# A decode block (attention with a cached K and V, then a Mish MLP): query projection head by head, last output-projection group in 4+3+1 rows, mean from column sums first, bias in two bf16 parts

## The chip, the cores and the metric

One NeuronCore of a Trainium2 chip runs the whole program. The time is device time in microseconds (us) of one execution. The traces have one row of work for each engine: the tensor engine (PE), the vector engine (DVE), the scalar engine (ACT) and the sync engine (SP, which issues nearly all the DMAs); they also tell what ended an engine's idle time before an instruction. "PEld" is the loading of weights into PE.

A *ratio* below is the mean time of a kernel's fast runs over the mean time of the fast runs of the kernel before in the same rounds. It is therefore not quite the ratio of the medians that I quote.

## The reference, cut to what matters

```python
# x: (4,1,640); K, V: (4,32,4096,128) bf16; wq: (640,4096); wo: (4096,640); w1: (640,1728); w2: (1728,640)
def A(x, k_cache, v_cache, wq, wo):            # attention, one query per sequence
    q = (x @ wq) split into 32 heads of 128
    p = softmax(q . k_cache * 128**-0.5)
    return concat_heads(p . v_cache) @ wo
def B(x, w1, b1, w2):                          # MLP with Mish
    h = x @ w1 + b1
    return (h * tanh(softplus(h))) @ w2
h   = x + A(layernorm(x), ...)
out = h + B(layernorm(h), ...)
```

K and V are 134 MB each in bf16 and every byte is read once, so nearly all of the run is reading them.

## The kernel before: the parts that the change touches

There are 16 K tiles and 16 V tiles of 8.4 MB. They pass through three big SBUF slots, loaded from one DMA queue in program order. After the last V tile the queue brings wo (five loads), w1 (three) and w2 (four).

```python
# which rows of the weights come in one load
WOS = [(k, 0, G) for k in range(NHG - 1)] + [(NHG - 1, 0, G - 2), (NHG - 1, G - 2, G)]   # 8, 8, 8, 6, 2 rows
W1S = (0, 2, DC - 1, DC)                                                             # 2 + 2 + 1 rows
W2S = (0, 6, 10, 12, FM)
...
# head: query projection, 40 matmuls, then 128 small selection matmuls that spread q over partitions
for hg in range(NHG):
    for b in range(N):
        for g in range(G):
            mm(red[:, (2 + hg) % 4, b * Dh : (b + 1) * Dh],
               sel[r, b, SE - PG * g : SE - PG * g + P], q_all[r, g * Dh : (g + 1) * Dh],
               g == 0, g == G - 1, ("qb", hg) if done else None)
...
# tail, on PE: wo, then mean and mean of squares, then w1 with the bias put in as an fp32 matmul
wo_mm(0); o_mm(NT - 1); l_mm(hg); wo_mm(1); a_mm(hg); ...; wo_mm(2); wo_mm(3)    # -> y
pe.need("st")
for k in range(2):                       # k=0: y, k=1: y*y
    ...
    mm(s_ps[k], ones_d[:, :], st[:, k, :, :], True, True, ("s", k))
pe.need("cen")
for c0, c1 in zip(W1S, W1S[1:]):
    if c1 == DC - 1:
        pe.need("b1s")
        mm(red[:, 2, 0 : FC * N], ident_f[:, :], b1s[:, :, :], False, False)     # fp32
    pe.need(("w1", c0))
    ...                                  # 14 matmuls for each row c of w1
# tail, on DVE: st <- y; mu[k] <- sum over chunks of s_ps[k]; cen <- st - mu[0]; ...
```

In the tail, `wo_mm` are the matmuls with wo; `o_mm`, `l_mm` and `a_mm` finish the attention of the last heads for them. After w1 come a fixed chain (h1, exp on ACT, five DVE instructions, `act`), the w2 matmuls and the output.

The softmax here doesn't subtract the row's maximum and nothing guards it: scores larger than these inputs give would overflow.

## Time and profile before

| | before |
|---|---|
| median time | 663.01 us (4 runs, 662.70 to 663.21) |
| span of the profiled run | 661.1 us |
| bytes moved, mean rate | 283.5 MB, 429 GB/s |
| PE, DVE busy | 60%, 62% |
| last K or V, wo, w1, w2 loads landed | 634.89, 647.14, 652.55, 657.52 us |
| the three w1 parts landed | 649.26, 651.50, 652.55 us |

(A "landing" is the last of a load's completion events in the trace, from the span's start.)

The page of the kernel before: the span in 40 slices, then the chain that ended last.

```profile
DMA  9999999999999999999999999999999999999997
GB/s 390 437 444 440 441 417 420 441 436 442 433 436 416 444 436 432 436 440 420 436 436 436 436 436 440 416 444 433 432 440 436 420 440 432 432 440 440 408 420 293
...
## 4 chain that ended last, share of the span: by engine, by line
DMA 3%; PE 3%; DVE 0%; SPq 0%; issue 0%; ACT 0%
DMA slotB<-in_A_wo_dram 3%; PE red L708 1%; PE pv L708 1%; PE red L718 0%; PE y_ps L708 0%; SPq L250 0%; PE misc L708 0%; DVE tb L694 0%; DVE o_bf L704 0%; ACT ta L428 0%; DVE act L697 0%; DVE tb L683 0%; DVE h L671 0%; DVE tb L691 0%; DVE cen L633 0%
```

The DMA row is at 9 tenths in every slice but the last, and the rate stays between 408 and 444 GB/s between the first and the last slice. The transfers are the limit. The chain of waits reaches back to a DMA, the load of wo, and what follows it in the chain is the tail.

The timeline of the kernel before, from its last wo matmuls to the end of the w1 stage (start, length, engine, line, operation, output<-input; in brackets the engine's idle time before it and what ended that).

```profile
646.49 1.73 PE L708 MATMUL y_ps<-a_t,slotB 128*128 128x4 bf16 x40 [0.54 <-DMA slotB<-in_A_wo_dram]
648.26 0.18 DVE L613 COPY st<-y_ps 128x20 f32<-128x20 f32 x1 [4.49 <-PE y_ps L708]
...
648.49 0.62 PE L708 MATMUL misc<-st,ones_d 128*128 128x20 f32 x2 [0.27 <-DVE st L613]
...
648.94 0.59 PE L708 MATMUL pv<-st,ones_d 128*128 128x20 f32 x2
649.14 0.18 DVE L624 TENSOR_REDUCE mu<-misc 128x4 f32<-128x20 f32 x1 [0.50 <-PE misc L708]
649.36 0.18 DVE L633 TENSOR_TENSOR cen<-st,mu 128x20 bf16<-128x20 f32 x1
...
649.59 1.92 PE L708 MATMUL red<-cen,slotB 128*64 128x4 bf16 x28
...
651.37 0.66 PE L708 MATMUL red<-b1s,ident_f 128*128 128x56 f32 x2
...
651.96 2.95 PE L708 MATMUL red<-cen,slotB 128*64 128x4 bf16 x42
...
654.94 0.22 DVE L671 TENSOR_TENSOR h<-red,rstd 128x56 f32<-128x56 f32 x1 [4.26 <-PE red L708]
```

The last wo row landed at 647.14 us, but PE had been waiting since 645.94 for a load of six rows and started its 40 matmuls only at 646.49. The sums y are ready at 648.26. Then a copy, a matmul, a reduce and a subtract follow one another until the centred row `cen` is ready at 649.54. The w1 matmuls run without a gap from 649.59 to 654.91, with 0.64 us in between for the fp32 bias. PE never waits for w1: every part of it had landed before PE came to it.

### The profile page before, as it was taken

How to read it: one execution, taken by the hardware profiler on the slowest of the kernel's cores; microseconds unless marked ns; L12 is line 12 of the kernel's file. 1: busy time of each engine (PE TensorE's matmuls, PEld its weight loads, DVE VectorE, ACT ScalarE, POOL GpSimd, SP SyncE). 2: the span in 40 equal slices, each digit the busy share in tenths (PEclk: the TensorE clock that was granted, in tenths of full speed). 3: DMA queues.
4: the chain of work that ended last, by engine and by line, in shares of the span. 5: the costliest groups of instructions: out<-in, count | busy, mean ns of one | idle time of the engine just before them, and what ended most of it. 6: DMA issues, size and time to landing. Idle time of an engine off the chain costs nothing. (4 is left out here: it accounts for less than half of the span.)

```text
span 661.1 us, 5195 instructions
## 1 busy us (share of the span) xinstructions
PE 396.9 (60%) x2747; PEld 80.8 (12%) x1787; DVE 406.9 (62%) x252; ACT 41.6 (6%) x158; POOL 2.6 (0%) x14
## 2 busy tenths in 40 slices
PE   0856658568317595738407485838434656765767
PEld 0600000101101010101100010000110001010246
DVE  1077988386048779757218798849306798848612
ACT  0200000000000000000000000000000000000011
POOL 1000000000000000000000000000000000000000
PEclk9768787968658697958767887888876879797965
DMA  9999999999999999999999999999999999999997
GB/s 390 437 444 440 441 417 420 441 436 442 433 436 416 444 436 432 436 440 420 436 436 436 436 436 440 416 444 433 432 440 436 420 440 432 432 440 440 408 420 293
DMA packets 6978, 283.50 MB, mean 429 GB/s; under 512 B 1012, under 2 KB 1208, under 8 KB 2232
## 3 DMA queue, kind: packets, MB, share of 16 engines
q1 hardware_dynamic: 6640, 283.27, 99.2%
q8 instruction: 7, 0.11, 0.1%
q10 hardware_dynamic: 328, 0.09, 0.1%
q14 instruction: 3, 0.02, 0.0%
HBM read 283.35 MB, written 0.01 MB: 429 GB/s over the span
## 5 line engine op out<-in xcount | busy, mean ns | idle before, releaser
L515 DVE TENSOR_TENSOR slotA<-slotA,q_bc 128x8192 bf16<-128x8192 bf16 x32 | 140.6, 4416 | 104.3 <-DMA slotA<-in_A_k_cache_dram 104.3
L515 DVE TENSOR_TENSOR slotB<-slotB,q_bc 128x8192 bf16<-128x8192 bf16 x32 | 140.7, 4418 | 16.7 <-DMA slotB<-in_A_k_cache_dram 16.7
L526 DVE TENSOR_REDUCE s_f<-red 128x64 f32<-128x1024 f32 x64 | 78.0, 1219 | 97.7 <-PE red L718 97.6
L718 PE MATMUL red<-slotA,ident 128*128 128x512 bf16 x480 | 136.4, 447 | 0.0
L718 PE MATMUL red<-slotB,ident 128*128 128x512 bf16 x480 | 127.1, 424 | 0.0
L708 PE MATMUL red<-slotA,ident 128*128 128x512 bf16 x32 | 14.6, 456 | 118.9 <-PEq L49 118.9
L708 PE MATMUL pv<-slotC,e 128*32 128x512 bf16 x768 | 53.4, 439 | 36.9 <-PEq L49 33.9
L708 PE MATMUL red<-slotB,ident 128*128 128x512 bf16 x32 | 14.1, 440 | 87.5 <-PEq L49 87.5
L394 ACT ACTIVATE ex<-s_f 128x64 bf16<-128x64 f32 x64 | 16.4, 256 | 503.1 <-DVE s_f L526 503.1
L540 DVE TENSOR_TENSOR e<-ex,hmask 128x512 bf16<-128x512 bf16 x64 | 39.8, 684 | 0.0
L708 PEld LDWEIGHTS pv<-slotC,e 128*32 128x32 bf16 x768 | 22.7, 108 | 96.2 <-issue 82.9
L708 PEld LDWEIGHTS red<-slotA,ident 128*128 128x128 bf16 x32 | 3.2, 99 | 187.7 <-issue 187.6
L708 PEld LDWEIGHTS red<-slotB,ident 128*128 128x128 bf16 x32 | 3.1, 98 | 170.6 <-issue 170.6
L708 PEld LDWEIGHTS o_ps<-pv_sb,selo 128*32 128x32 f32 x136 | 13.5, 109 | 63.0 <-issue 62.9
L708 PE MATMUL o_ps<-pv_sb,selo 128*32 128x128 f32 x136 | 18.0, 276 | 0.0
L708 PE MATMUL pv<-slotA,e 128*32 128x512 bf16 x256 | 14.6, 380 | 0.4 <-PEq L49 0.4
L404 ACT COPY pv_sb<-pv 128x512 f32<-128x512 f32 x16 | 9.4, 586 | 70.4 <-PE pv L708 70.4
L394 ACT ACTIVATION_READ_ACCUMULATOR ex<-s_f 128x1 f32 x64 | 11.9, 186 | 0.0
L708 PE MATMUL red<-q_all,sel 32*128 32x128 bf16 x128 | 10.3, 273 | 0.8 <-PEq L49 0.8
L708 PEld LDWEIGHTS red<-q_all,sel 32*128 32x128 bf16 x128 | 10.1, 124 | 1.6 <-issue 1.6
L708 PEld LDWEIGHTS pv<-slotA,e 128*32 128x32 bf16 x256 | 7.0, 97 | 23.4 <-issue 17.7
L565 DVE RECIPROCAL rl<-misc 32x1 f32<-32x1 f32 x4 | 0.6, 151 | 14.3 <-PE misc L708 14.3
(96 smaller groups left out, 77.8 us busy)
## 6 DMA issues: line engine op xcount, KB each, us to landing
slotC<-in_A_v_cache_dram SPq DMA_DIRECT2D x2, 4096.0 KB, 40.6
slotC<-in_A_wq_dram SPq DMA_DIRECT2D x1, 5120.0 KB, 15.9
slotB<-in_A_wo_dram SPq DMA_DIRECT2D x3, 1280.0 KB, 17.7
slotB<-in_B_w_dram SPq DMA_DIRECT2D x2, 864.0 KB, 25.0
slotB<-in_A_wo_dram SPq DMA_DIRECT2D x1, 960.0 KB, 22.1
slotA<-in_B_w_dram SPq DMA_DIRECT2D x1, 960.0 KB, 25.2
slotA<-in_B_w_dram SPq DMA_DIRECT2D x1, 640.0 KB, 22.4
slotB<-in_B_w_dram SPq DMA_DIRECT2D x1, 432.0 KB, 26.4
```

Source lines behind the costliest of these rows:

```text
L394: lambda: a.activation(out=ex[:, sl], in_=s_f[:, sl], func=ACT.Exp, scale=SCALE, accum_out=rs[:, b, s : s + 1],),
L404: lambda: a.copy(out=pv_sb[:, :, :].rearrange("p r d -> p (r d)"), in_=pv[:, :]),
L515: lambda: v.tensor_tensor(out=t, in0=t, in1=q_bc[:, hg, b, :].unsqueeze(1).to_broadcast([P, RS, Dh]), op=ALU.mult,),
L526: lambda: v.tensor_reduce(out=s_f[:, s * RS : (s + 1) * RS], in_=red[:, k : k + 2, :].rearrange("p k (r c) -> p (k r) c", c=CW), axis=AX.X ...
L540: lambda: v.tensor_tensor(out=e[:, sl, :], in0=ex[:, sl].unsqueeze(2).to_broadcast([P, RS, G]), in1=hmask[:, :].unsqueeze(1).to_broadcast( ...
L565: dv.do(lambda: v.reciprocal(out=rl[:, :], in_=l_ps), ("rl", hg), DV)
L708: lambda: nc.tensor.matmul(out_, lhsT=lhsT, rhs=rhs, start=start, stop=stop, skip_group_check=skip),
L718: return t.add_instruction(mybir.InstMatmult(name=nc.get_next_instruction_name(), engine=mybir.EngineType.PE, ins=[t.lower_ap(rhs), t.lowe ...
```

## The change

The intent is to shorten the two places where the program is serial: the head (128 selection matmuls become 4) and the tail (a smaller last load of wo, one step less to the mean, a cheaper bias).

```diff
-    WOS = [...] + [(NHG - 1, 0, G - 2), (NHG - 1, G - 2, G)]
+    WOS = [...] + [(NHG - 1, a, b) for a, b in ((0, 4), (4, 7), (7, G))]
 # head: 40 projection matmuls write all heads into one bank; then
-        for hg in range(NHG):
-            for b in range(N):
-                for g in range(G):
-                    mm(red[:, (2 + hg) % 4, b * Dh : (b + 1) * Dh], sel[r, b, ...], q_all[r, ...], ...)
+        for b in range(N):
+            mm(red[:, (1 + b) % 4, :], sel[:, b * G : (b + 1) * G, :], q_all[:, :], True, True, ("qb", b))
 # tail, DVE
+        ysum <- tensor_reduce(y_ps over chunks)          # first, so that the mean needs no reduce afterwards
         st <- y_ps;  sq <- st * st
-        mu[0] <- tensor_reduce(s_ps[0]);  cen <- st - mu[0]
+        cen <- st - m_ps                                 # straight from PSUM
 # tail, PE
-            mm(s_ps[k], ones_d, st[:, k, :, :], ...)     # k = 0, 1
+        mm(m_ps, ones_d, ysum, True, True, "mean")
+        mm(sq_ps, ones_d, sq, True, True, "sqm")
-            if c1 == DC - 1:
-                mm(red[:, 2, ...], ident_f, b1s, ...)    # fp32, before the second w1 part
+            if c1 == DC:
+                for part in (b1_hi, b1_lo):              # b1s = b1_hi + b1_lo, both bf16
+                    mm(red[:, 2, ...], ident, part, ...) # before the last w1 part
```

More of the change, by code (lines that the diff above doesn't have):

```diff
@@ L121 @@
     book = Book()
-    WSEM = ["WQ", "WT"] + [f"W{k}" for k in range(12)]
+    WSEM = ["WQ", "WT"] + [f"W{k}" for k in range(13)]
     for s in ["PE", "DV", "DVP", "DVA", "AC", "ACP", "PO", "KA", "KB", "VA", "VC", "V2", "X", "S", "OUT0", "OUT1", "FIN"] + WSEM:
@@ L175 @@
     ln1 = sb("ln1", (N, D), BF16, setup, topC)
-    lnT = sb("lnT", (P, DC, QD), BF16, setup, topC)
+    lnT = sb("lnT", (P, DC, 2 * QD - N), BF16, setup, topC)
     xT = sb("xT", (P, DC, N), BF16, setup, topC)
-    q_all = sb("q_all", (P, QN), BF16, setup, topC)
-    SE = P - PG
-    sel_f = sb("sel_f", (P, N), FP32, setup, topC)
-    sel = sb("sel", (P, N, SE + P), BF16, setup, topC)
+    q_all = sb("q_all", (P, NHG * Dh), BF16, setup, topC)
+    sel_f = sb("sel_f", (P, N, G), FP32, setup, topC)
+    sel = sb("sel", (P, BG, PG), BF16, setup, topC)
     stats = sb("stats", (N, 2, nc.vector.BN_STATS_DIM), FP32, setup, topC)
@@ L192 @@
     ones_d = sb("ones_d", (P, P), FP32, tail, topA)
-    ident_f = sb("ident_f", (P, P), FP32, tail, topA)
     zeros = sb("zeros", (P, OC), BF16, tail, topA)
-    st = sb("st", (P, 2, DC, N), FP32, tail, topA)
-    mu = sb("mu", (P, 2, N), FP32, tail, topA)
+    ysum = sb("ysum", (P, N), FP32, tail, topA)
+    st = sb("st", (P, DC, N), FP32, tail, topA)
+    sq = sb("sq", (P, DC, N), FP32, tail, topA)
+    mu = sb("mu", (P, N), FP32, tail, topA)
+    esq = sb("esq", (P, N), FP32, tail, topA)
     cen = sb("cen", (P, DC, N), BF16, tail, topA)
@@ L202 @@
     b1s = sb("b1s", (P, FC, N), FP32, tail, topA)
+    b1_hi = sb("b1_hi", (P, FC, N), BF16, tail, topA)
+    b1_lo = sb("b1_lo", (P, FC, N), BF16, tail, topA)
     h_hi = sb("h_hi", (P, DC, N), BF16, tail, topA)
@@ L224 @@
     a_ps = misc[:, 128 : 128 + G * N].rearrange("p (j n) -> p j n", n=N)
-    s_ps = [t[:, 0 : DC * N] for t in (misc, pv)]
+    m_ps = misc[:, 0:N]
+    sq_ps = pv[:, 0 : DC * N]
     h1_ps = red[:, 2, 0 : FC * N].rearrange("p (j n) -> p j n", n=N)
@@ L230 @@
     out_rows = out.rearrange("b s d -> (b s) d")
-    WOS = [(k, 0, G) for k in range(NHG - 1)] + [(NHG - 1, 0, G - 2), (NHG - 1, G - 2, G)]
+    WOS = [(k, 0, G) for k in range(NHG - 1)] + [(NHG - 1, a, b) for a, b in ((0, 4), (4, 7), (7, G))]
     W1S = (0, 2, DC - 1, DC)
@@ L303, in sync_prog @@
                 k_load(i + 1)
-            sp.need(("PV", i - 1) if hg else ("qb", NHG - 1))
+            sp.need(("PV", i - 1) if hg else ("qb", N - 1))
             v_load(i)
@@ L345, in pool_prog @@
         po.do(lambda: g.memset(lnT[:, :, :], 0.0), "lnz", "PO")
-        po.do(lambda: g.memset(sel[:, :, :], 0.0), "selz", "PO")
         po.do(lambda: g.memset(selo[:, :, :], 0.0), "seloz", "PO")
@@ L351, in pool_prog @@
         po.do(lambda: g.memset(zeros[:, :], 0.0), "zeros", "PO")
-        po.do(lambda: g.tensor_copy(out=ident_f[:, :], in_=ident[:, :]), "ident_f", "PO")
     def act_prog():
@@ L365, in act_prog @@
         )
-        for h in range(2):
-            ac.need(("q", h))
-            ac.do(
-                lambda: a.copy(out=q_all[:, h * 512 : (h + 1) * 512], in_=red[:, h, :]),
-                ("qa", h), "ACP",
-            )
-        for hg in range(NHG):
-            ac.need(("qb", hg))
+        ac.need("q")
+        ac.do(lambda: a.copy(out=q_all[:, :], in_=red[:, 0, :]), "qa", "ACP")
+        for b in range(N):
+            ac.need(("qb", b))
             ac.do(
                 lambda: a.copy(
-                    out=q_bc[:, hg, :, :].rearrange("p b d -> p (b d)"), in_=red[:, (2 + hg) % 4, :]
+                    out=q_bc[:, :, b, :],
+                    in_=red[:, (1 + b) % 4, :].rearrange("p (h d) -> p h d", d=Dh),
                 ),
-                ("qc", hg), "AC",
+                ("qc", b), "AC",
             )
@@ L446, in dve_prog @@
             lambda: v.tensor_reduce(
-                out=sel_f[:, :],
-                in_=ident[:, :].rearrange("p (h m) -> p m h", h=CG)[:, 0:N, :],
+                out=sel_f[:, :, :],
+                in_=ident[:, :].rearrange("p (k g b) -> p b g k", k=CG, b=N),
                 axis=AX.X, op=ALU.add,
@@ L482, in dve_prog @@
         )
-        dv.need("delta_f", "selz")
+        dv.need("delta_f")
         dv.do(lambda: v.tensor_copy(out=hmask[:, :], in_=hmask_f[:, :]), "hmask", DV)
@@ L487, in dve_prog @@
             lambda: v.tensor_copy(
-                out=sel[:, :, SE : SE + PG],
-                in_=sel_f[:, :].unsqueeze(2).to_broadcast([P, N, PG]),
+                out=sel[:, :, :], in_=sel_f[:, :, :].rearrange("p b g -> p (b g)").unsqueeze(2).to_broadcast([P, BG, PG]),
             ),
@@ L503, in dve_prog @@
         dv.need("tpl", "lnz")
-        dv.do(lambda: v.tensor_copy(out=lnT[:, :, 0:N], in_=tpl[:, :, :]), "lnT", DVP)
+        dv.do(lambda: v.tensor_copy(out=lnT[:, :, QD - N : QD], in_=tpl[:, :, :]), "lnT", DVP)
         dv.need("tpx")
@@ L507, in dve_prog @@
         dv.do(lambda: v.memset(rsm[:, :, :], 1.0), ("rsm", -1), DVP)
-        dv.need(("qc", NHG - 1), "hmask")
+        dv.need(("qc", N - 1), "hmask")
         def mult(i, s):
@@ L612, in dve_prog @@
         dv.need("y", "zeros")
-        dv.do(lambda: v.tensor_copy(out=st[:, 0, :, :], in_=y_ps[:, :, :]), "st", DV)
+        dv.do(
+            lambda: v.tensor_reduce(
+                out=ysum[:, :], in_=y_ps.rearrange("p c n -> p n c"), axis=AX.X, op=ALU.add
+            ),
+            "ysum", DVP,
+        )
+        dv.do(lambda: v.tensor_copy(out=st[:, :, :], in_=y_ps[:, :, :]), "st", DV)
         dv.need("st")
         dv.do(
-            lambda: v.tensor_tensor(
-                out=st[:, 1, :, :], in0=st[:, 0, :, :], in1=st[:, 0, :, :], op=ALU.mult
-            ),
+            lambda: v.tensor_tensor(out=sq[:, :, :], in0=st[:, :, :], in1=st[:, :, :], op=ALU.mult),
@@ L619, in dve_prog @@
             "sq", DVP,
         )
-        for k in range(2):
-            dv.need(("s", k))
-            dv.do(
-                lambda: v.tensor_reduce(
-                    out=mu[:, k, :], in_=s_ps[k].rearrange("p (c n) -> p n c", n=N),
-                    axis=AX.X, op=ALU.add,
-                ),
-                ("mu", k), DV,
-            )
-            if k == 0:
-                dv.need(("mu", 0))
-                dv.do(
-                    lambda: v.tensor_tensor(
-                        out=cen[:, :, :], in0=st[:, 0, :, :],
-                        in1=mu[:, 0, :].unsqueeze(1).to_broadcast([P, DC, N]), op=ALU.subtract,
-                    ),
-                    "cen", DVP,
-                )
-                dv.do(
-                    lambda: v.tensor_tensor(
-                        out=msq[:, :], in0=mu[:, 0, :], in1=mu[:, 0, :], op=ALU.mult
-                    ),
-                    "msq", DV,
-                )
@@ L645, in dve_prog @@
-        dv.need(("mu", 1))
+        dv.need("mean")
         dv.do(
             lambda: v.tensor_tensor(
-                out=var[:, :], in0=mu[:, 1, :], in1=msq[:, :], op=ALU.subtract
-            ),
+                out=cen[:, :, :], in0=st[:, :, :],
+                in1=m_ps.unsqueeze(1).to_broadcast([P, DC, N]), op=ALU.subtract,
+            ),
+            "cen", DVP,
+        )
+        dv.do(lambda: v.tensor_copy(out=mu[:, :], in_=m_ps), "mu", DV)
+        dv.need("mu")
+        dv.do(
+            lambda: v.tensor_tensor(out=msq[:, :], in0=mu[:, :], in1=mu[:, :], op=ALU.mult),
+            "msq", DV,
+        )
@@ L650, in dve_prog @@
+        dv.need("sqm")
+        dv.do(
+            lambda: v.tensor_reduce(
+                out=esq[:, :], in_=sq_ps.rearrange("p (c n) -> p n c", n=N), axis=AX.X, op=ALU.add
+            ),
+            "esq", DV,
+        )
+        dv.need("esq", "msq")
+        dv.do(
+            lambda: v.tensor_tensor(out=var[:, :], in0=esq[:, :], in1=msq[:, :], op=ALU.subtract),
             "var", DV,
         )
-        dv.do(lambda: v.tensor_copy(out=h_hi[:, :, :], in_=st[:, 0, :, :]), "h_hi", DV)
+        dv.do(lambda: v.tensor_copy(out=h_hi[:, :, :], in_=st[:, :, :]), "h_hi", DV)
@@ L658, in dve_prog @@
             ),
-            "b1s", DVP,
+            "b1s", DV,
         )
+        dv.need("b1s")
+        dv.do(lambda: v.tensor_copy(out=b1_hi[:, :, :], in_=b1s[:, :, :]), "b1_hi", DV)
         dv.do(lambda: v.reciprocal(out=rstd[:, :], in_=std2[:, :]), "rstd", DV)
@@ L664, in dve_prog @@
             lambda: v.tensor_tensor(
-                out=h_lo[:, :, :], in0=st[:, 0, :, :], in1=h_hi[:, :, :], op=ALU.subtract
+                out=h_lo[:, :, :], in0=st[:, :, :], in1=h_hi[:, :, :], op=ALU.subtract
             ),
-            "h_lo", DVP,
+            "h_lo", DV,
+        )
+        dv.need("b1_hi")
+        dv.do(
+            lambda: v.tensor_tensor(
+                out=b1_lo[:, :, :], in0=b1s[:, :, :], in1=b1_hi[:, :, :], op=ALU.subtract
+            ),
+            "b1_lo", DVP,
         )
@@ L745, in pe_setup @@
         pe.need("lnT", "wq")
-        for h in range(2):
+        GK = G // CG
+        for r in range(GK):
             for c in range(DC):
-                for hg in range(NHG):
-                    o = hg * QN + h * 512
-                    mm(
-                        red[hg * QD : (hg + 1) * QD, h, :], lnT[:, c, :], wq[:, c, o : o + 512],
-                        c == 0, c == DC - 1,
-                        ("q", h) if c == DC - 1 and hg == NHG - 1 else None,
-                    )
-        pe.need(("qa", 0), ("qa", 1))
-        for hg in range(NHG):
-            for b in range(N):
-                for g in range(G):
-                    r = slice(hg * QD, (hg + 1) * QD)
-                    done = b == N - 1 and g == G - 1
-                    mm(
-                        red[:, (2 + hg) % 4, b * Dh : (b + 1) * Dh],
-                        sel[r, b, SE - PG * g : SE - PG * g + P],
-                        q_all[r, g * Dh : (g + 1) * Dh],
-                        g == 0, g == G - 1, ("qb", hg) if done else None,
-                    )
+                for k in range(CG):
+                    g = k * GK + r
+                    mm(
+                        red[k * QD : (k + 1) * QD, 0, :], lnT[:, c, QD - N * (g + 1) : 2 * QD - N * (g + 1)],
+                        wq[:, c, :].rearrange("p (h g d) -> p g h d", g=G, d=Dh)[:, g, :, :],
+                        r == 0 and c == 0, r == GK - 1 and c == DC - 1,
+                        "q" if r == GK - 1 and c == DC - 1 and k == CG - 1 else None,
+                    )
+        pe.need("qa", "sel")
+        for b in range(N):
+            mm(
+                red[:, (1 + b) % 4, :], sel[:, b * G : (b + 1) * G, :].rearrange("p g q -> p (g q)"),
+                q_all[:, :], True, True, ("qb", b),
+            )
     def fold(i, s):
@@ L863, in pe_tail @@
         a_mm(hg)
-        pe.need("ident_f", ("e", NT - 1, NS - 1))
+        pe.need("zeros", ("e", NT - 1, NS - 1))
         mm(red[:, 2, 0 : FC * N], ident[:, :], zeros[:, 0 : FC * N], True, False)
@@ L868, in pe_tail @@
         wo_mm(3)
-        pe.need("st")
-        for k in range(2):
-            if k:
-                pe.need("sq")
-            mm(
-                s_ps[k], ones_d[:, :], st[:, k, :, :].rearrange("p c n -> p (c n)"), True, True,
-                ("s", k),
-            )
+        pe.need("ysum")
+        mm(m_ps, ones_d[:, :], ysum[:, :], True, True, "mean")
+        pe.need("sq")
+        mm(sq_ps, ones_d[:, :], sq[:, :, :].rearrange("p c n -> p (c n)"), True, True, "sqm")
         pe.need("cen")
         for c0, c1 in zip(W1S, W1S[1:]):
-            if c1 == DC - 1:
-                pe.need("b1s")
-                mm(
-                    red[:, 2, 0 : FC * N], ident_f[:, :], b1s[:, :, :].rearrange("p j n -> p (j n)"),
-                    False, False,
-                )
+            if c1 == DC:
+                pe.need("b1_lo")
+                for part in (b1_hi, b1_lo):
+                    mm(
+                        red[:, 2, 0 : FC * N], ident[:, :], part[:, :, :].rearrange("p j n -> p (j n)"),
+                        False, False,
+                    )
             pe.need(("w1", c0))
@@ L896, in pe_tail @@
                     )
-        pe.need("h_lo")
+        pe.need("h_lo", "h_hi")
         for part in (h_hi, h_lo):
```

## The prediction

> **What bounds the kernel.** The DMA stream. The page's slices show DMA at 9 tenths in 39 of 40; 283.5 MB move at 429 GB/s over a span of 661.1 us, and the trace's packets, in 5 us bins, show 428 to 434 GB/s from 15 to 630 us, with no gap. The Trainium skill (DMA: Bandwidth & Descriptors, "Where 436 GB/s comes from") gives 435.2 GB/s as the fabric ceiling; this trace agrees (434). So bytes fix when each load lands: w1 in three parts at 649.26, 651.50 and 652.55 us, the last row of w2 at 657.52 us. Only the work behind those landings can shorten the span.
>
> **The head.** In the timeline, 40 query matmuls run from 16.0 us, then 128 selection matmuls (10.3 us); the last copy ends at 32.2 us. The first K tile lands only at 36.1 us and DVE starts at 36.2 (the waits: DVE <- DMA, 27.3 us). With 4 selection matmuls I estimate q near 24 us. The first V load is issued near 23 instead of 31.6 us, but queues behind the second K tile (landed 55.4 us). Worth: 0.0 us.
>
> **The tail, step by step** (timeline after 640 us; granted clock 0.5 there):
> - wo: PE ends the third group at 645.94, waits for six rows (landed 646.35), runs 40 matmuls, y at 648.22. With 4+3+1, four rows land about 645.6 (0.378 us a row), so PE runs on; y near 647.74: -0.48 us.
> - mean: copy, matmul, reduce, subtract take 648.26 to 649.54. Column sums first drop the reduce between matmul and subtract (0.21 us with its hand-over). cen would be ready at 648.8-648.9: some -0.7 us in all.
> - bias: the fp32 pair costs 0.64 us (651.32 to 651.96); two bf16 matmuls some 0.15-0.2 us, before the last w1 part.
>
> That is some 1.2 us off the compute chain, but w1 is in the way. Its first part lands at 649.26 plus about 0.02 for the extra, smaller load, so PE starts near 649.42 (0.14 us from landing to start, as measured for wo), not 648.9; it ends 28 matmuls near 651.2 and waits for the second part, landed 651.52, start about 651.66, against 651.96 before. The 42 matmuls that remain take 2.87 us and now the bias pair is among them: h1 sums end near 654.75 against 654.91. The chain behind (h1, exp, DVE chain, w2, out) is unchanged. So 1.2 us shrinks to about 0.15 us; the rest becomes PE waiting on DMA.
>
> **Prediction.** 663.0 us, range 662.3 to 663.8. Faster by over 2%: 0.005; within 2%: 0.99; slower: 0.005.
>
> **What shows each step right or wrong.** Head: V load issued near 23 us, DVE's first multiply still at 36.2. wo: y_ps matmuls nearly continuous, y near 647.7. Mean: cen near 648.8, then a new wait "PE red <- DMA slotB<-in_B_w" of some 0.4 us, and a second of some 0.4 us before the second w1 part. The chain of waits should name the w1 load where before it named the wo load. Bias: two short bf16 matmuls instead of the fp32 pair. Landings unchanged within 0.1 us; DMA share the same.
>
> **What would make it wrong.** Landings of w1 that move (the extra load has 1280-byte rows; the sync engine's last issues already take 12 us); a warmer clock in the tail; a chip-to-chip difference in DMA rate over 0.1%, which swamps 0.15 us; a bias pair that stalls PE longer than I think.

## The result, and the profile after

| | before | after |
|---|---|---|
| median time | 663.01 us (4 runs) | 662.47 us (4 runs, 662.41 to 663.31) |
| ratio, 95% interval | | 0.9995 [0.9978, 1.0013] |
| median in a second set of rounds | 662.90 us (9 runs) | 662.43 us (5 runs) |
| ratio there | | 0.9991 [0.9977, 1.0004] |
| span of the profiled run | 661.1 us | 661.0 us |

The change is worth about half a microsecond, less than 0.1%. Both intervals contain a ratio of 1. The traces resolve more than the times do.

The page of the changed kernel.

```profile
DMA  9999999999999999999999999999999999999997
GB/s 386 444 440 444 421 408 445 437 441 437 429 420 440 436 436 436 440 428 424 444 432 432 440 428 424 444 432 433 444 436 432 424 440 428 440 440 428 412 418 303
...
## 4 chain that ended last, share of the span: by engine, by line
DMA 4%; PE 3%; SPq 0%; DVE 0%; issue 0%; ACT 0%
DMA slotB<-in_B_w_dram 4%; PE red L724 1%; PE red L714 1%; PE pv L714 1%; SPq L254 0%; DVE tb L700 0%; DVE o_bf L710 0%; ACT ta L427 0%; DVE h L677 0%; DVE act L703 0%; DVE tb L689 0%; DVE tb L697 0%
```

The DMA row is the same. The chain that ended last no longer ends at wo's load: it ends at a load of w1.

The timeline of the changed kernel over the same stretch.

```profile
644.59 3.56 PE L714 MATMUL y_ps<-a_t,slotB 128*128 128x4 bf16 x80
...
648.19 0.18 DVE L612 TENSOR_REDUCE ysum<-y_ps 128x4 f32<-128x20 f32 x1 [3.81 <-PE y_ps L714]
...
648.42 0.59 PE L714 MATMUL misc<-ysum,ones_d 128*128 128x4 f32 x2 [0.27 <-DVE ysum L612]
...
648.87 0.59 PE L714 MATMUL pv<-sq,ones_d 128*128 128x20 f32 x2
649.05 0.18 DVE L625 TENSOR_TENSOR cen<-st,misc 128x20 bf16<-128x20 f32 x1 [0.39 <-PE misc L714]
...
649.76 3.93 PE L714 MATMUL red<-cen,slotB 128*64 128x4 bf16 x56 [0.30 <-DMA slotB<-in_B_w_dram]
...
651.78 1.83 PEld L714 LDWEIGHTS red<-cen,slotB 128*64 128x64 bf16 x28 [0.21 <-DMA slotB<-in_B_w_dram]
...
653.58 0.23 PE L714 MATMUL red<-b_lo,ident 128*128 128x56 bf16 x1
...
653.74 1.10 PE L714 MATMUL red<-cen,slotB 128*64 128x4 bf16 x14
...
654.87 0.22 DVE L677 TENSOR_TENSOR h<-red,rstd 128x56 f32<-128x56 f32 x1 [3.92 <-PE red L714]
```

Each planned step is there. The wo matmuls run on through the smaller loads, and y is ready 0.63 us after the last wo landing (647.56) instead of 1.12. `cen` is ready 1.66 us after that landing instead of 2.40. The bias takes 0.25 us instead of 0.64. But PE waits for w1 twice. The first wait, 0.30 us, ends with the landing at 649.63. The second, 0.21 us on the weight-load row, ends with the landing at 651.73. From the last wo landing to the end of the w1 stage the chain went from 7.77 us to 7.28 us, so half a microsecond was kept.

Why then did the spans differ by only 0.1 us? Because the last wo row itself landed at 647.56 in this trace and at 647.14 in that of before. The stream wanders by this much from run to run, as the table in the next section shows. In this pair the shift was there before the tail: wq, the first big load, landed at 16.36 us after the change and at 15.88 before. From wq's landing to the end of the span it is 645.2 us before and 644.7 after, half a microsecond less.

The head. The timeline of the kernel before, at the selection matmuls, the last query copy and the first multiply by q.

```profile
21.22 10.31 PE L708 MATMUL red<-q_all,sel 32*128 32x128 bf16 x128 [0.78 <-PEq L49]
...
31.56 0.33 SPq L250 DMA_DIRECT2D slotC<-in_A_v_cache_dram  x1
31.57 0.59 ACT L375 CAST q_bc<-red 128x512 bf16<-128x512 f32 x1 [2.38 <-PE red L708]
...
36.20 8.76 DVE L515 TENSOR_TENSOR slotA<-slotA,q_bc 128x8192 bf16<-128x8192 bf16 x2 [27.27 <-DMA slotA<-in_A_k_cache_dram]
```

The same stretch in the timeline of the changed kernel.

```profile
21.73 1.86 PE L714 MATMUL red<-q_all,sel 128*128 128x512 bf16 x4 [0.78 <-PEq L49]
...
22.35 2.05 ACT L373 CAST q_bc<-red 128x512 bf16<-128x512 f32 x4 [0.77 <-PE red L714]
...
23.62 0.33 SPq L254 DMA_DIRECT2D slotC<-in_A_v_cache_dram  x1
...
35.87 8.76 DVE L513 TENSOR_TENSOR slotA<-slotA,q_bc 128x8192 bf16<-128x8192 bf16 x2 [26.38 <-DMA slotA<-in_A_k_cache_dram]
```

q is ready at 24.4 us instead of 32.2, and the first V load is issued 8 us sooner. DVE uses none of it. It waits for the first K tile in both.

### The profile page after: what moved, and what is told of

It is laid out like the page before. It is cut to its first block, busy times and chain, and to the rows that moved or that the text cites. A ratio compares the mean times of both kernels' runs of the same rounds, so it can differ in the third digit from the quotient of the medians.

```text
span 661.0 us, 4948 instructions
## 1 busy us (share of the span) xinstructions
PE 386.6 (58%) x2623; PEld 70.5 (11%) x1663; DVE 407.4 (62%) x255; ACT 40.7 (6%) x157; POOL 1.7 (0%) x12
## 5 line engine op out<-in xcount | busy, mean ns | idle before, releaser
L393 ACT ACTIVATION_READ_ACCUMULATOR ex<-s_f 128x1 f32 x64 | 11.9, 186 | 0.0
L714 PE MATMUL red<-slotC,lnT 128*32 128x512 bf16 x40 | 4.5, 629 | 6.7 <-PEq L49 6.7
L714 PE MATMUL y_ps<-a_t,slotB 128*128 128x4 bf16 x160 | 7.0, 179 | 0.2
## 6 DMA issues: line engine op xcount, KB each, us to landing
slotB<-in_A_wo_dram SPq DMA_DIRECT2D x3, 1280.0 KB, 15.9
slotB<-in_A_wo_dram SPq DMA_DIRECT2D x1, 480.0 KB, 20.3
```

Source lines behind the costliest of these rows:

```text
L393: lambda: a.activation(out=ex[:, sl], in_=s_f[:, sl], func=ACT.Exp, scale=SCALE, accum_out=rs[:, b, s : s + 1],),
L714: lambda: nc.tensor.matmul(out_, lhsT=lhsT, rhs=rhs, start=start, stop=stop, skip_group_check=skip),
```

## The experiments

Theory A is that of the prediction: the head has slack and is worth nothing; the tail's compute chain became about 1.1 us shorter; in this order of loads, w1's landings take part of that back. The rivals were these. B: the tail's steps cost what they save. C: the last landing alone sets the end, whatever the tail computes. C': finer loads help by themselves. D: it is the shorter head that gains. E: the query stage is on the critical path.

Readings from the traces, in us. "wo" is the last wo landing; the columns after it are read from the timelines.

| kernel | wo | y ready | cen ready | first w1 matmul | w1 stage ends | wo to w1 end | span |
|---|---|---|---|---|---|---|---|
| before | 647.14 | 648.26 | 649.54 | 649.59 | 654.91 | 7.77 | 661.1 |
| head_only | 647.34 | 648.45 | 649.73 | 649.78 | 655.07 | 7.73 | 661.3 |
| sel_half (old tail) | 647.35 | 648.48 | 649.76 | 649.82 | 655.12 | 7.77 | 661.3 |
| tail_only | 647.45 | 648.07 | 649.11 | 649.70 | 654.71 | 7.26 | 660.9 |
| after | 647.56 | 648.19 | 649.22 | 649.77 | 654.84 | 7.28 | 661.0 |
| after_again | 647.70 | 648.61 | 649.64 | 649.88 | 654.93 | 7.23 | 661.1 |
| before_w1first | 652.69 | 653.79 | 655.07 | 655.12 | 660.43 | 7.74 | 666.6 |
| after_w1first | 652.95 | 653.58 | 654.62 | 654.79 | 659.70 | 6.75 | 665.9 |
| after_w1five | 647.65 | 648.58 | 649.61 | 649.78 | 655.07 | 7.42 | 661.3 |

From the end of the w1 stage to the end of the span it is 6.2 us in all of them, so the last columns carry the argument. Each row is one trace.

### The head alone, the tail alone, and both again

`head_only` is the kernel before with only the head's part of the change. `tail_only` is the changed kernel with the head of before. `after_again` is the changed kernel once more, on the same chip. Each had five rounds.

```diff
 # head_only: before, plus
+        for b in range(N):
+            mm(red[:, (1 + b) % 4, :], sel[:, b * G : (b + 1) * G, :], q_all[:, :], True, True, ("qb", b))
 # tail_only: before, plus WOS 4+3+1, ysum/mean, b1_hi/b1_lo
```

> The kernel before with the head-by-head query projection alone. Theory A (the query stage has slack behind the first K tile and the DMA queue): the first V load is issued near 22 to 24 us instead of 31.6, q is ready near 24 us, and the time stays within 0.2 us of before. Rival D, formed from the traces so far: all three traces of kernels with the old head have an instruction fetch of 16 KB at 26.8 to 27.1 us and the first K tile landing at 36.1 to 36.4 us; all three with the new head have no such fetch and land it at 35.7 to 35.8 us, so the shorter head program gives the stream some 0.4 us: then this run lands the first K tile near 35.7 us, and is 0.2 to 0.5 us faster than before, which would be most of the difference that the changed kernel showed.

> The changed kernel with the old query stage. Theory A: as fast as the changed kernel within 0.2 us, 0.1 to 0.5 us faster than before. Rival D: the fetch at 27 us is back, the first K tile lands near 36.2 us, and the time is within 0.2 us of before.

> The changed kernel again, beside the parts on the same chip: 0.2 to 0.5 us faster than before by both; its first K tile lands at 35.7 us, its PE waits for w1 twice.

| | median | ratio, 95% interval |
|---|---|---|
| before | 662.90 us | |
| head_only | 662.98 us | 1.0001 [0.9987, 1.0014] |
| tail_only | 662.56 us | 0.9995 [0.9981, 1.0009] |
| after_again | 662.43 us | 0.9991 [0.9977, 1.0004] |

The head alone gives nothing, and the tail alone gives 0.34 us of the 0.47 by medians. The intervals (0.13% either way, 0.9 us) do not resolve these differences. The chain lengths do: 7.73 us with the old tail, 7.26 and 7.23 with the new one.

Rival D was half right, in a way that taught something. The instruction fetch that it named (16 KB at 26.9 us, 1.07 us long) is in `tail_only` and not in `head_only`, as it said. From the landing of wq to that of the first K tile it takes 19.9 us with the fetch and 19.4 us without. But `head_only` is no faster: if the fetch is what delays that landing (the two heads differ in more than the fetch), nobody was short of it.

### Where the slack of the head ends

`sel_x2` is the kernel before with every selection matmul done twice; `sel_half` has half of them done twice.

```diff
-                for g in range(G):
+                for x in range(2 * G):            # sel_x2; sel_half: range(-(G // 2), G)
+                    g = x % G                     # sel_half: g = x % (G // 2) if x < 0 else x
```

> The kernel before with every selection matmul of the query stage done twice (256 instead of 128), so q is ready some 10.3 us later, near 42.5 us, and the first multiply starts 6.3 us later than now. Theory A: the third K tile's load is issued near 69.4 us, still ahead of the landing of the first V tile (74.7 us), so the queue never empties and the time is within 0.6 us of before. Rival E (the query stage is on the critical path): some 6 to 10 us slower.

This one missed. It took 669.40 us against 662.90, ratio 1.0096 [1.0078, 1.0115], 6.5 us slower (two executions, one round). That is where rival E had put it.

The timeline of `sel_x2`, at the first multiply and the next load of K.

```profile
48.05 8.76 DVE L515 TENSOR_TENSOR slotA<-slotA,q_bc 128x8192 bf16<-128x8192 bf16 x2 [39.12 <-ACT q_bc L375]
...
53.00 4.94 PE L718 MATMUL red<-slotA,ident 128*128 128x512 bf16 x15
...
59.12 3.40 PE L718 MATMUL red<-slotA,ident 128*128 128x512 bf16 x15
...
74.94 0.33 SPq L250 DMA_DIRECT2D slotA<-in_A_k_cache_dram  x1
```

The 128 added matmuls did not take 10.3 us, as I had estimated from the 128 of before, but 15.9. q was ready at 48.0 us and not at 42.5, so the third K tile's load went out at 74.94 us. The first V tile, the last load that was queued, had landed at 74.68. The queue had run empty: this load landed 23.2 us after its issue, where 19.3 us is a tile's time in a full stream. So I repeated the test with half of the addition.

For that I had put the slower matmuls down to a low clock. The profile seems to say otherwise. Busy time by stretch of `sel_x2` (stretch, its length, busy us and instruction count of PE, PEld, DVE, ACT and POOL; then the granted clock, the DMA share, GB/s).

```profile
31.00:47.00 16.00, 16.00 (x162) 16.00 (x160) 0.00 (x0) 1.17 (x2) 0.00 (x0) 1.00 1.05 452
```

This 1.00 is no reading. The trace of `sel_x2` holds no clock record before 56.11 us, and the view counts missing records as full clock. The pace of the matmuls tells the clock. In before, the record stands at 1.00 from 20.27 to 23.68 us and then at 0.50; its selection matmuls follow one another at about 0.05 us up to 23.7 us and at 0.092 to 0.093 after that. In `sel_x2` they follow at 0.092 to 0.107 all along. The 512-column matmuls after them agree: they follow at 0.43 us until the record begins, with 1.00, at 56.11 us, and at 0.22 after it (hence 4.94 us for the first 15 shown and 3.40 for the later 15). So the low clock was the right reason, and the estimate from before was too low because its 128 matmuls had a start at full clock, which `sel_x2` never had.

> The kernel before with half of the selection matmuls done twice (192 instead of 128). The doubled ones of sel_x2 took 15.9 us for 128 at the low clock, so 64 take some 7.9 us: q ready near 40.1 us, first multiply 3.9 us later than before, third K tile's load issued near 67.0 us. In sel_x2 that load was issued at 74.9 us and landed 23.2 us later, 3.9 us over the 19.3 us of a full queue, so it must be issued by some 70.8 us to cost nothing. Theory A (slack of the query stage about 11.7 us in all, nothing to gain from it in before): time within 0.3 us of before. Rival E (each us of the first multiply's start costs a us): 3.9 us slower.

`sel_half` took 663.08 us against 662.96, ratio 1.0001 [0.9985, 1.0016]. Its first multiply started at 38.8 us, 2.6 us later than in before (I had expected 3.9), its third K load went out at 65.74 us and landed at 93.98, as in before (94.00). So the head of before has slack: delaying the first multiply by 2.6 us costs nothing, and delaying it by 11.9 us costs 6.5. A head that is 8 us *faster* has nothing to give. This excludes E for the kernel as it was: E would have made `sel_half` 2.6 us slower, and its interval ends 1.1 us above before.

### The same change where w1 is not in the way

Both kernels, with w1's loads moved in front of the last wo group, five rounds each. The bytes are the same. The price is that the whole serial tail now follows a wo row that lands some 5.5 us later. What counts is the difference of the two.

```diff
         for n, (q, j0, j1) in enumerate(WOS):
+            if n == NHG - 1:
+                (the three loads of w1)
             load(sp, wo_sb[:, q, j0:j1, :], ...)
-        (the three loads of w1)
```

> The kernel before with the w1 loads moved ahead of the last wo group's, so that no w1 load is left to wait for after the last wo row; the bytes are the same. All theories: the last wo row lands some 5.2 us later (estimate: 2160 KB at 434 GB/s) near 652.5 us, and the whole compute chain (7.8 us from the last wo landing to the h1 sums, measured in before) comes behind it; h1 sums near 660.3 us, span near 666.5 us, so 0.8% slower than before. This kernel is the base line for the next one.

> The changed kernel with the same move of the w1 loads. Theory A (the tail's compute chain did become some 1.1 us shorter, and in the order of loads of the changed kernel most of it is turned into waits for w1): 1.0 to 1.3 us shorter than before_w1first, span near 665.3 us; from the last wo landing to the h1 sums some 6.7 us against 7.8; no PE wait for a w1 load. Rival B (the steps cost as much as they save, the chain is no shorter): within 0.3 us of before_w1first. Rival C (the end is set by the last w2 landing and the tail's compute does not count): both of these runs equal to before, within 0.3 us.

`before_w1first` took 668.11 us, ratio 1.0078 [1.0065, 1.0092]; `after_w1first` took 667.16 us, ratio 1.0065 [1.0051, 1.0079]. The difference of the medians is 0.95 us, and the five runs of each do not overlap (667.99 to 668.20 and 666.89 to 667.83 us); it was 0.5 us in the usual order.

The timeline of `before_w1first`, where y, `cen` and the end of the w1 stage are read.

```profile
653.79 0.18 DVE L614 COPY st<-y_ps 128x20 f32<-128x20 f32 x1 [8.60 <-PE y_ps L709]
...
654.89 0.18 DVE L634 TENSOR_TENSOR cen<-st,mu 128x20 bf16<-128x20 f32 x1
...
660.47 0.22 DVE L672 TENSOR_TENSOR h<-red,rstd 128x56 f32<-128x56 f32 x1 [4.26 <-PE red L709]
```

The timeline of `after_w1first`.

```profile
652.58 0.96 PE L715 MATMUL y_ps<-a_t,slotB 128*128 128x4 bf16 x20 [0.16 <-DMA slotB<-in_A_wo_dram]
653.58 0.18 DVE L613 TENSOR_REDUCE ysum<-y_ps 128x4 f32<-128x20 f32 x1 [8.18 <-PE y_ps L715]
...
654.26 0.59 PE L715 MATMUL pv<-sq,ones_d 128*128 128x20 f32 x2
654.44 0.17 DVE L626 TENSOR_TENSOR cen<-st,misc 128x20 bf16<-128x20 f32 x1 [0.39 <-PE misc L715]
...
654.79 3.77 PE L715 MATMUL red<-cen,slotB 128*64 128x4 bf16 x56
...
658.60 1.10 PE L715 MATMUL red<-cen,slotB 128*64 128x4 bf16 x14
...
659.73 0.22 DVE L678 TENSOR_TENSOR h<-red,rstd 128x56 f32<-128x56 f32 x1 [3.38 <-PE red L715]
```

The w1 stage runs without a wait for DMA, and the chain is 6.75 us against 7.74: 0.99 us shorter. B and C are excluded: B expected a difference within 0.3 us, C expected no change from the order of loads.

The sum of its parts, from the table: y comes 0.47 us sooner after the last wo landing (0.63 against 1.10). `cen` follows y in 1.04 us instead of 1.28, so 0.24 us are saved. But w1 starts 0.17 us after `cen` instead of 0.05, so 0.12 of these are lost. The w1 stage with the bias takes 4.91 us instead of 5.31, so 0.40 us are saved.

`after_again` shows the limit from the other side. There y came 0.91 us after the last wo landing instead of 0.63. The four fp32 matmuls of `o_mm` (eight in the profile) took 1.92 us and not 1.06, so PE came late to the wo rows. Yet the w1 stage ended no later (7.23 us after the wo landing, against 7.28): a delay of y of 0.3 us was swallowed by the wait for w1.

The cause of the late `o_mm` is the granted clock: from 640.6 to 642.6 us it was 1.00 in `after` and 0.50 in `after_again`. The Trainium skill (TensorE: Matmul & The Clock Gate, "Part 1: The HAM clock gate") says that the halved clock is the default and that about 3.4 us of sustained work release it. In `after` that fits: work began at 635.4 us behind the last V load, and the trace's clock record shows the full clock from 639.85 to 643.26. In `after_again` PE was at work from 635.5 on as well, and the record shows 0.50 to the end. What differed is the kind of work. The record changes only in steps of 3.41 us. In the step that ended at 639.85, the 512-column matmuls of the attention ran for 2.58 us in `after`; in the one that ended at 640.39 in `after_again` they ran for 2.14, and PE spent the rest on matmuls with 4 columns (wo). The last section has this for all traces. So the tail's compute chain can change by 0.86 us at this place from run to run without any change of the program.

### Finer w1 loads

If two waits for w1 eat half the gain, then w1 in smaller parts should give some of it back, and should do nothing for the kernel before. Five rounds each.

```diff
-    W1S = (0, 2, DC - 1, DC)
+    W1S = tuple(range(DC + 1))
```

> The kernel before with w1 loaded in five parts of one row each instead of 2+2+1. In before the PE never waits for w1 (every part had landed before the PE came to it). Theory A: nothing to gain, within 0.15 us of before, at most some 0.1 us worse for the extra loads. Rival C' (finer loads help by themselves): faster by over 0.3 us.

> The changed kernel with w1 in five parts. Theory A: the two waits for w1 (together some 0.6 us and a later start than cen allows) go, h1 sums some 0.7 to 0.9 us sooner, w2 then waits for its last rows near 657.8 us; span 0.5 to 0.8 us shorter than the changed kernel, near 660.3 us, or 662.0 us in time. Rivals B and C: within 0.2 us of the changed kernel.

`before_w1five` took 663.19 us, ratio 1.0004 [0.9991, 1.0018]. It was not faster, which speaks against C' (the interval alone would leave room for 0.3 us); in its trace the chain from the last wo landing to the w1 end is 8.14 us, against 7.77. But 0.33 us by medians is above the 0.15 I allowed. `after_w1five` took 662.52 us, ratio 0.9993 [0.9979, 1.0007]; the expected gain of 0.5 to 0.8 us over the changed kernel did not come.

The chain that ended last of `after_w1five`, in order of time (start, length, what). After the last V landing at 635.36 us it names no DMA at all.

```profile
635.50 3.60 PE pv L714 x32
639.10 1.69 PE y_ps L714 x40
640.79 1.85 PE o_ps L714 x8
...
645.39 3.16 PE y_ps L714 x80
...
648.81 0.59 PE misc L714 x2
...
649.85 5.23 PE red L714 x72
...
655.11 0.23 DVE h L677
```

Two things ate it. First, the waits for w1 were gone, but the chain of PE work behind the last *V* landing was right behind them: wo's 80 matmuls start at 645.18, run on without waiting for a load and end 0.9 us after the last wo landing. In this trace, too, `o_mm` ran at half clock (1.92 us), so up to 0.86 us of that lateness may be the clock's; the two were not taken apart. Second, the w1 stage itself grew from 4.91 us (`after_w1first`) to 5.28, and in the kernel before from 5.31 to 5.69. Each part begins with the 64-column remainder of w1, and in the trace each turn to 64 columns and back costs 0.13 to 0.15 us where matmuls otherwise follow at 0.06. Two more parts bring four such turns, some 0.3 us of the 0.37. The Trainium skill (TensorEngine Tiling (Array Packing), "Key Properties") says that changing the tiling mode drains the tensor engine; the gaps stand at exactly these places. That draining is their cause was not tested.

### The squares' matmul later, and the last V tile split later

`sqlate_w1first` is `after_w1first` with the matmul of the squares behind the first w1 part. `five_sqlate` is `after_w1five` with the same move. `five_sqlate_v34` loads the last V tile in 3/4 + 1/4 as well, so that less PE work follows its landing.

```diff
-        mm(sq_ps, ones_d[:, :], sq[:, :, :], True, True, "sqm")
         ...
+            if c0 == 0:                       # after the matmuls of the first w1 part
+                mm(sq_ps, ones_d[:, :], sq[:, :, :], True, True, "sqm")
 # five_sqlate_v34 also:
-        n = SLOT // 2 if i == NT - 1 else SLOT
+        n = SLOT * 3 // 4 if i == NT - 1 else SLOT
```

> after_w1first with the matmul of the squares moved behind the first w1 part on the tensor engine. In after_w1first the first w1 matmul started 0.17 us after the centred row was done, against 0.05 us in before_w1first, and I put that down to the squares' fp32 matmul that stands before it in the engine's order. If so, the gap falls to some 0.05 us and h1 sums come 0.1 us sooner from the last wo landing (6.65 us instead of 6.75; the matmul itself, some 0.45 us, is then paid inside the w1 stage, which may eat this gain and more: then 6.9 to 7.1 us). If the gap stays at 0.17 us, its cause is another.

> The changed kernel with w1 in five parts and the squares' matmul behind the first of them. Against after_w1five (662.52 us): the squares' matmul fills a time in which the engine waits for the next w1 row, so up to 0.1 us sooner or equal. Against the changed kernel: 0 to 0.4 us sooner.

> As five_sqlate, with the last V tile loaded in 3/4 and 1/4 instead of two halves. From the traces: after the last V landing (635 us) the tensor engine is at work without a break until y in four of the six tail traces (fp32 matmuls at half clock), so wo no longer waits for its loads there. A later split leaves 16 matmuls instead of 32 (1.8 us less) behind that landing, y then comes 0.5 us after the last wo landing instead of 0.9. Theory A': y - last wo landing 0.5 to 0.6 us, w1 bound by its landings alone, span 0.4 to 0.7 us below the changed kernel's, near 660.5 us, time near 661.9 us. Rival: no change from five_sqlate within 0.15 us.

`sqlate_w1first` took 667.84 us, ratio 1.0071 [1.0057, 1.0085]. The first w1 matmul now starts 0.06 us after `cen` (0.17 in `after_w1first`), so the squares' matmul was indeed the cause of that delay. But the chain grew to 7.10 us from 6.75, because the matmul now takes 0.58 us inside the w1 stage, which grew by 0.47 us (5.38 against 4.91). Before `cen` it had run for the most part while PE waited for DVE anyway. It was in the better place.

`five_sqlate` took 663.01 us, ratio 0.9997 [0.9984, 1.0011]: about 0.5 us *later* than the changed kernel's two medians, where I expected 0 to 0.4 sooner, and about 0.4 us later than `after_w1five` where I expected up to 0.1 sooner (each against its own before). It has the same fault, 0.59 us inside a stage that waits for nothing; its chain from the wo landing is 7.79 us against 7.42. `five_sqlate_v34` took 662.56 us in the same rounds, ratio 0.9992 [0.9978, 1.0005]. Its y came 0.64 us after the last wo landing (647.41 to 648.05) instead of 0.89 in `five_sqlate`, as the theory of the V landing says. Its span of 661.1 us missed the 660.5 that I expected, and the squares' 0.59 us are still in it.

None of these versions beats the changed kernel. Five w1 parts with the later V split but with the squares' matmul left in its place was not run. I estimate it at some 0.3 us below the changed kernel: `five_sqlate_v34` is 0.40 us below before by medians, the squares' place would give 0.37 (7.79 less 7.42), and the changed kernel is 0.47 below before. That stays open.

## Why the prediction was right

The time (663.0 us predicted, 662.47 measured, range 662.3 to 663.8) and "within 2%" hold. That alone says little: the range also holds the time of before, 663.01 us, and the time came out 0.54 us lower where 0.15 was forecast. So the mechanism is what counts, point by point:

- **The DMA stream is the bound: right.** The rate is 429 GB/s in both, and the chain of waits ends at a load in both.
- **The head is worth 0.0 us: right, shown.** `head_only` is at 1.0001, and `sel_half` shows that the slack is real. The predicted times (V load near 23 us, q near 24) were met at 23.6 and 24.4.
- **wo: -0.48 us: right.** It was -0.49 in the pair of the result and -0.47 in the pair with w1 first.
- **Mean: "some -0.7 us in all" to `cen`: right** (-0.74). What I had left out is that the squares' matmul stands between `cen` and w1 and costs 0.12 us of it.
- **Bias: 0.15 to 0.2 us instead of 0.64:** it was 0.25.
- **"Some 1.2 us off the compute chain":** 0.99 us, in `after_w1first`.
- **"1.2 us shrinks to about 0.15 us": the right mechanism, the wrong size.** Both waits for w1 came as named (PE idle for 0.30 and 0.21 us, where some 0.4 each was forecast), and the chain of waits named the w1 load. But about 0.5 us was kept, not 0.15. I had placed the second w1 landing 4.36 us after the last wo landing, from the one trace that I had. In five of the six other traces with that order of loads and 2+2+1 rows it is 4.10 to 4.17 (`sel_x2` has 4.39). I had also added 0.14 us from that landing to the start; measured were 0.05. Together that is 0.3 us.
- **"Landings unchanged within 0.1 us": wrong.** The last wo landing is at 647.14 to 647.70 us in the six traces of the table with the usual order and three w1 parts, though their streams carry the same bytes up to there. That scatter is as large as the gain, and it is why spans and single times could not show the gain.

## What to carry to other kernels

When a kernel is bound by one stream of loads, shortening the compute behind a load pays only up to the next load's landing. Write down the landings next to the compute chain before the change, and count each saving only as far as the next one. To see what a change to the compute is worth by itself, move the loads out of its way in both versions and compare those two: here this turned 0.5 us in the noise into 0.95. And before splitting loads more finely, look at what else each part carries (here two changes of tile shape), and at which chain comes next when the wait is gone.

## What the Trainium skill lacked or had wrong

- TensorE: Matmul & The Clock Gate, "Part 1: The HAM clock gate" says that about 3.4 us of sustained work release the clock. In `after_again` PE was busy without a break from 635.5 to 642.6 us and the granted clock stayed at 0.50 all that time and to the end; in `after`, with the same work from 635.4 on, it rose at 639.85. The page does not say which work counts. In the 14 traces here the clock records change only in steps of 3.41 us, and 1135 steps at half clock can be followed into the next one. The full clock came after 391 of them; in each of these, 512-column matmuls ran for 2.58 us or more. It did not come after the other 744; in each of those they ran for 2.58 us or less, even where PE was busy for all 3.41 us with matmuls of 4 columns. This is read from one family of kernels, and the ends of matmuls are modelled.
- DMA: Bandwidth & Descriptors, "Where 436 GB/s comes from" says that for HBM to SBUF the HBM side (about 358 GB/s) binds. With one core running this program, its loads moved at 434 GB/s from 60 to 600 us, just under the page's own fabric ceiling (435.2). The page's remark that 358 is for two cores streaming stands before that section; the sentence misleads a reader who has one core at work.
- Runtime: NRT & Kernel Launch, "Instruction fetch mechanics" calls the cost of fetching the next 16 KiB of instructions mostly hidden; it has no figure for what a fetch takes from a stream of loads that is the bound. Here 16 KB at a time, each 0.9 to 1.4 us long, went through the DMA engines (the queues that the profile calls "instruction"). In the six traces with one in the first K tile that tile landed 19.8 to 20.3 us after wq, in the eight without it 19.4. That the fetch is the cause is inferred from this alone; the six also have the old head.
- TensorEngine Tiling (Array Packing), "Key Properties" says that a change of tiling mode drains the engine but gives no figure. At half clock, the turn from 128 to 64 output columns and back took 0.13 to 0.15 us each, where matmuls followed at 0.06; whether the drain is the reason was not tested.
- FP8 and Floating Point Precision, "TensorE Precision Notes" gives fp32 four passes. The profile shows each fp32 matmul as two weight loads and two matmuls, and does not show whether one of these holds two passes; the 56-column bias took 0.64 us in fp32 and 0.25 us as two bf16 parts, so the gain was 2.6 times.
